# One core, 2,196 tasks in a written order: the order written anew, with 49 fewer tasks that only keep TensorE running

## The chip, the cores and the metric

The kernel runs on one core of a Trainium2 chip. A core has TensorE (PE in the profile: matmuls; PEld: the loading of its stationary operand), VectorE (DVE), ScalarE (ACT), GpSimd (POOL) and SyncE (SP, which here only issues DMAs). The engines run each its own queue in order and wait for one another by semaphores. The metric is the device time of one execution in microseconds; three runs of the kernel before took 638.27, 638.80 and 639.24 us, median 638.8 us.

## What is computed

A delta rule over 768 steps in each of 32 heads (4 batches of 8 heads, head size 48), and its output, seen as 3,072 tokens of 384 features, goes through a feed-forward block whose gate is h cos h:

```python
k_n = k / (np.linalg.norm(k, axis=-1, keepdims=True) + 1e-06)
for t in range(S):
    y[:, :, t] = np.einsum('bhd,bhde->bhe', q[:, :, t], state)
    v_old = np.einsum('bhde,bhd->bhe', state, kt)
    state = state + bt[:, :, :, None] * np.einsum('bhd,bhe->bhde', kt, vt - v_old)
...
h = x @ w_in          # x: 3072 x 384, w_in: 384 x 2048
g = h * np.cos(h)
return g @ w_out      # w_out: 2048 x 384
```

The weights arrive as 64-bit floats and are narrowed on the chip.

## The kernel before

**Delta rule.** The 768 steps are cut into 24 units n of 32 steps. For a unit, `turn` transposes keys and queries on TensorE (units 0 to 7; later units are loaded in blocks and turned on VectorE), `turn_out` evicts them, `gram` multiplies keys with keys and queries (line 673), `gram_keys` and `gram_queries` scale and mask the products on VectorE. Each unit then needs the inverse of a triangular 32 x 32 matrix per head:
- units 0 and 1 by `double`: six levels of small matmuls (L757), in two halves (`par`) each, and between the levels `double_copy` on ScalarE and `double_turn` and `double_add` on VectorE (L765 to L777);
- units 2 and 3 by a half-size substitution, with `solve_half`, `between` and `solve`;
- units from 4 on in pairs m = n // 2 by substitution on GpSimd: `gram_put` writes the matrices to DRAM, `gram_get` reads both units' back in another layout (L852), `inv` m, 0 to 6 does 31 columns of two instructions (L877, L884), `put` writes the result (L889) and `get` reads it per unit (L908).

Then come `state` (product with the running state, L928), `right` (VectorE), `solve` (L994, L1000), `solve_out`, `update` (L1025) and `update_out` (the new state), `within` and `within_out` (the unit's outputs) and `features` and `features_out` (transposed, as input of the feed-forward block). `update_out` n must precede `state` n + 1: this is the only chain through all units.

**Feed-forward block.** Two units make one tile p of 256 tokens, 12 tiles in all. Tiles 0 and 1 go through plain matmuls (`hidden`, L1097); the others through 20 shared products (`layer`, L1271). `turns`, `rest`, `cos` and `gate` (ScalarE and VectorE in turn) make h cos h; `out` (L1353; L1295 for tile 0) is the second matmul, from tile 1 on in seven products of two parts. `x_sum`, `left`, `right`, `in_sums` are sums of operands on VectorE or GpSimd.

**Weights.** 28 pieces: `weights` t loads, `split` t (ScalarE, two instructions), `shift` t (VectorE), `add` t (GpSimd) narrow it. `hidden` 0, f needs `add` up to 3 (f // 2 % 4) + 2, and `out` 0, 0, k needs `add` 12 to 15 + 4k.

**Order.** All this is a list of tasks. Each has a key such as `("gram", 5)`. `Order.LINE` lists the numbers of all tasks; `run` emits them in this order, and since each engine's queue is in order, the list fixes what stands behind what on every engine. It also fixes which buffer a task gets. `Order.OTHER` holds the keys of tasks that go to a second engine instead of their first: DMAs to ScalarE's queue instead of SyncE's, `inv`, `left`, `right`, `in_sums` and `x_sum` to the other of VectorE and GpSimd.

**Unread products.** `keep_warm` (lines 491 to 493) multiplies two tiles of ones into `p_out`, which nobody reads. `WARM_FIRST` = 5 of them are emitted ahead of the list, and `WARMS` tasks `("warm", i)` stand in the list. Each `warm` task that comes after the first `out` task emits nothing (`out_begun` is then not empty). Before, 31 of the 56 stand ahead of the first `out`.

Of the kernel before, what the change touches and what calls it, by code (L numbers as in the profile page):

```python
# [59 lines left out]
class Order:  # L60

    OTHER = {
        ('gram_put', 2), ('q', 3), ('gram_get', 1), ('inv', 1, 0), ('put', 1), ('gram_put',
        4), ('gram_put', 5), ('v', 7), ('v', 8), ('v', 9), ('blocks', 11, 1), ('gram_put',
        11), ('put', 5), ('v', 13), ('put', 6), ('gram_put', 15), ('gram_get', 7), ('get',
        15), ('v', 16), ('blocks', 16, 0), ('blocks', 16, 1), ('gram_put', 16), ('blocks',
        18, 1), ('k', 19), ('blocks', 19, 0), ('gram_get', 9), ('get', 19), ('gram_put',
        20), ('v', 21), ('gram_put', 21), ('put', 10), ('gram_put', 22), ('v', 23),
        ('gram_put', 23), ('gram_get', 11), ('right', 4, 4), ('left', 1, 1, 0), ('left', 1,
        3, 0), ('left', 1, 3, 1), ('store', 1, 0), ('x_sum', 2, 'd'), ('x_sum', 2, 'n'),  # L70
        ('x_sum', 2, 'm'), ('x_sum', 2, 'e'), ('x_sum', 2, 'k'), ('x_sum', 2, 'g'),
        ('x_sum', 2, 'i'), ('x_sum', 2, 'l'), ('x_sum', 2, 'f'), ('x_sum', 2, 'b0'),
        ('left', 2, 4, 1), ('left', 2, 3, 1), ('x_sum', 3, 'd'), ('x_sum', 3, 'n'),
        ('x_sum', 3, 'm'), ('x_sum', 3, 'e'), ('x_sum', 3, 'k'), ('x_sum', 3, 'g'),
        ('x_sum', 3, 'i'), ('x_sum', 3, 'l'), ('x_sum', 3, 'h'), ('x_sum', 3, 'b0'),
        ('left', 3, 4, 1), ('left', 3, 3, 1), ('x_sum', 4, 'd'), ('x_sum', 4, 'm'),
        ('x_sum', 4, 'g'), ('x_sum', 4, 'i'), ('left', 4, 3, 0), ('left', 4, 3, 1),
        ('store', 4, 0), ('x_sum', 5, 'd'), ('x_sum', 5, 'e'), ('x_sum', 5, 'l'), ('x_sum',
        5, 'h'), ('x_sum', 5, 'b0'), ('left', 5, 2, 0), ('left', 5, 4, 1), ('left', 5, 3,
        0), ('left', 5, 3, 1), ('store', 5, 0), ('x_sum', 6, 'd'), ('x_sum', 6, 'g'),  # L80
        ('x_sum', 6, 'l'), ('x_sum', 6, 'f'), ('x_sum', 6, 'b0'), ('left', 6, 1, 0),
        ('left', 6, 4, 0), ('store', 6, 1), ('x_sum', 7, 'd'), ('x_sum', 7, 'm'), ('x_sum',
        7, 'g'), ('x_sum', 7, 'i'), ('x_sum', 7, 'f'), ('x_sum', 7, 'h'), ('x_sum', 7,
        'b0'), ('left', 7, 4, 0), ('left', 7, 4, 1), ('left', 7, 3, 1), ('x_sum', 8, 'd'),
        ('x_sum', 8, 'm'), ('x_sum', 8, 'e'), ('x_sum', 8, 'k'), ('x_sum', 8, 'g'),
        ('x_sum', 8, 'l'), ('left', 8, 3, 0), ('store', 8, 0), ('store', 8, 1), ('x_sum', 9,
        'd'), ('x_sum', 9, 'm'), ('x_sum', 9, 'e'), ('x_sum', 9, 'k'), ('x_sum', 9, 'i'),
        ('x_sum', 9, 'l'), ('x_sum', 9, 'b0'), ('left', 9, 1, 0), ('left', 9, 2, 0),
        ('left', 9, 1, 1), ('left', 9, 3, 0), ('store', 9, 0), ('x_sum', 10, 'k'), ('x_sum',
        10, 'i'), ('x_sum', 10, 'l'), ('x_sum', 10, 'h'), ('x_sum', 10, 'b0'), ('left', 10,  # L90
        1, 0), ('left', 10, 1, 1), ('left', 10, 4, 1), ('left', 10, 3, 0), ('left', 10, 3,
        1), ('store', 10, 0), ('x_sum', 11, 'd'), ('x_sum', 11, 'e'), ('x_sum', 11, 'k'),
        ('x_sum', 11, 'g'), ('x_sum', 11, 'f'), ('left', 11, 1, 0), ('left', 11, 2, 0),
        ('left', 11, 1, 1), ('left', 11, 3, 0), ('left', 11, 3, 1), ('store', 11, 1),
        ('store_right', 11), ('weights', 5), ('weights', 7), ('weights', 15), ('weights',
        16), ('weights', 18), ('weights', 20), ('weights', 22), ('weights', 23), ('weights',
        25), ('weights', 27)
    }

    WARM_FIRST, WARMS = 5, 56  # L100
    LINE = """
# [1845 lines left out]
```

## Time and profile before

| | us |
|---|---|
| median of three runs | 638.8 |
| span of the profiled execution, first to last instruction | 636.6 |
| TensorE busy, and of it the unread products (72 rows: 36 products of two rows) | 619.2, 23.1 |
| TensorE's weight loading busy | 576.2 |
| VectorE, GpSimd, ScalarE busy | 495.1, 435.8, 297.7 |

A row of the trace is one instruction: line of the kernel, engine, operation, the tiles it writes and reads, start and duration. An fp32 matmul of this kernel is two rows. "Idle before" is the time for which the engine had nothing to run ahead of a group, with what ended it.

### The profile page before, as it was taken

Reading aid. Unit: us, or ns where it says so; the run is one execution under the profiler, and the core shown is the slowest. Engines: PE = TensorE matmul, PEld = TensorE weight load, DVE = VectorE, ACT = ScalarE, POOL = GpSimd, SP = SyncE. Lnnn points to the kernel's source line nnn. Section 1 sums busy time; section 2 is a strip of 40 time slices with the busy share of each in tenths; the row PEclk is TensorE's granted clock in tenths of the full one; section 3 lists DMA queues with packets and bytes.
Section 4 is the critical chain, followed back from the end, with each engine's and each line's share of the span. In section 5 each row is a group of like instructions: output and inputs, shape, how many; then the busy total and the mean of one; then the engine's idle time right before and its main releaser. Section 6 shows DMA issues by size and latency. Waiting matters only on the chain.

```text
span 636.6 us, 24189 instructions
## 1 busy us (share of the span) xinstructions
PE 619.2 (97%) x10176; PEld 576.2 (90%) x10176; DVE 495.1 (78%) x1030; ACT 297.7 (47%) x528; POOL 435.8 (68%) x780
## 2 busy tenths in 40 slices
PE   5999989999999999999999999999999999999997
PEld 4877877987899999999999999999999999999997
DVE  5776656779998999887898888888888776566682
ACT  3457556562423444643642644733643553545440
POOL 5247788678788788887789888886884883112241
PEclk8899999999999999999999999999999999999999
DMA  8978656563651555435435344333304102000001
GB/s 173 221 171 213 121 155 146 93 118 60 116 68 22 94 90 99 60 67 104 61 70 98 56 73 90 58 57 67 74 3 81 44 1 43 19 2 26 1 25 26
DMA packets 209381, 50.37 MB, mean 79 GB/s; under 512 B 200920, under 2 KB 204280, under 8 KB 209272
## 3 DMA queue, kind: packets, MB, share of 16 engines
q1 hardware_dynamic: 161896, 35.03, 29.3%
q10 hardware_dynamic: 47072, 13.25, 10.0%
q8 instruction: 80, 1.31, 0.9%
q0 software_dynamic: 304, 0.54, 0.4%
q14 instruction: 29, 0.24, 0.1%
HBM read 38.55 MB, written 10.22 MB: 77 GB/s over the span
## 4 chain that ended last, share of the span: by engine, by line
PE 90%; DVE 3%; DMA 3%; ACT 1%; issue 1%; POOL 0%; SPq 0%; ACTq 0%; DVEq 0%
PE p_out L1353 29%; PE p_h L1271 27%; PE p_h L1097 6%; PE p_kq L928 4%; PE p_out L1295 3%; PE p_s L1025 3%; PE p_g L673 3%; PE p_h L757 3%; PE p_kq L1055 3%; PE p_u L1000 3%; PE p_out L493 2%; PE p_h L1353 2%; PE p_z L1076 1%; DMA kp<-in_k_dram 1%; PE p_t L640 1%
## 5 line engine op out<-in xcount | busy, mean ns | idle before, releaser
L877 POOL TENSOR_TENSOR part<-z,gb 128x126 f32<-128x126 f32 (+23 forms) x321 | 144.6, 451 | 46.7 <-DMA gb<-g_dr 21.2
L884 POOL TENSOR_TENSOR z<-z,part 128x126 f32<-128x126 f32 (+23 forms) x321 | 145.5, 453 | 25.1
L1353 PE MATMUL p_out<-w_out,g_ffn 128*128 128x192 f32 x672 | 121.9, 328 | 0.3 <-DVE o L1405 0.2
L1353 PEld LDWEIGHTS p_out<-w_out,g_ffn 128*128 128x128 f32 x672 | 107.7, 190 | 1.7 <-DVE o L1405 0.7
L1150 ACT ACTIVATE turns<-turns,halfpi 128x512 f32<-128x512 f32 x96 | 68.0, 719 | 55.7 <-DVE turns L1141 42.6
L1353 PE MATMUL p_out<-w_sum,g_ffn 128*128 128x192 f32 x496 | 89.7, 329 | 0.2 <-DVE o L1405 0.2
L1271 PE MATMUL p_h<-x_sum,w_in 128*128 128x128 f32 x640 | 84.0, 277 | 0.0
L1134 ACT ACTIVATE turns<-g_ffn,quarter_turn 128x512 int32<-128x512 f32 x70 | 49.8, 719 | 66.4 <-DVE g_ffn L1288 31.3
L1353 PEld LDWEIGHTS p_out<-w_sum,g_ffn 128*128 128x128 f32 x496 | 79.6, 190 | 1.2 <-issue 0.4
L1271 PEld LDWEIGHTS p_h<-x_sum,w_in 128*128 128x128 f32 x640 | 78.8, 192 | 1.1
L1288 DVE TENSOR_TENSOR g_ffn<-g_ffn,p_h 128x512 f32<-128x512 f32 x80 | 54.3, 681 | 17.3 <-PE p_h L1271 16.4
L1141 DVE SCALAR_TENSOR_TENSOR turns<-g_ffn,turns 128x512 f32<-128x512 f32 x70 | 55.3, 796 | 13.1 <-ACT turns L1134 13.0
L1068 ACT COPY y<-p_kq 32x384 f32<-32x384 f32 x96 | 45.2, 470 | 30.4 <-PE p_kq L1055 22.5
L1153 DVE TENSOR_TENSOR g_ffn<-turns,g_ffn 128x512 f32<-128x512 f32 x70 | 51.5, 745 | 3.8 <-ACT turns L1150 3.7
L1271 PE MATMUL p_h<-x_sum,in_sum 128*128 128x128 f32 x400 | 52.9, 277 | 0.0
L572 POOL TENSOR_TENSOR knrm<-ksum,halves 128x16 f32<-128x16 f32 (+1 forms) x14 | 36.4, 2602 | 23.9 <-DMA qp<-in_q_dram 12.6
L1271 PEld LDWEIGHTS p_h<-x_sum,in_sum 128*128 128x128 f32 x400 | 49.7, 192 | 0.8
L1405 DVE SCALAR_TENSOR_TENSOR o<-p_out,o 128x192 f32<-128x192 f32 x74 | 25.1, 351 | 28.4 <-PE p_out L1353 28.0
L1097 PE MATMUL p_h<-x_ffn,w_in 128*128 128x128 f32 x384 | 45.8, 277 | 0.0
L1097 PEld LDWEIGHTS p_h<-x_ffn,w_in 128*128 128x128 f32 x384 | 44.1, 192 | 1.2
L1271 PE MATMUL p_h<-x_ffn,w_in 128*128 128x128 f32 x320 | 42.4, 277 | 0.0
L1369 POOL TENSOR_TENSOR g_ffn<-g_ffn,g_ffn 128x512 f32<-128x512 f32 x18 | 25.8, 1442 | 22.5 <-PE p_out L1353 18.7
(168 smaller groups left out, 1071.3 us busy)
## 6 DMA issues: line engine op xcount, KB each, us to landing
g_ffn<-in_moe_w_in_dram SPq DMA_DIRECT2D x10, 512.0 KB
gb<-g_dr SPq DMA_DIRECT2D x14, 256.0 KB
vp<-in_v_dram SPq DMA_DIRECT2D x68, 48.0 KB
g_ffn<-in_moe_w_out_dram SPq DMA_DIRECT2D x8, 384.0 KB
g_ffn<-in_moe_w_out_dram ACTq DMA_DIRECT2D x8, 384.0 KB
kp<-in_k_dram SPq DMA_DIRECT2D x120, 24.0 KB
out_dram<-o SPq DMA_DIRECT2D x14, 192.0 KB
zt<-z_dr SPq DMA_DIRECT2D x72, 32.0 KB
```

Source lines behind the costliest of these rows:

```text
L572: nc.gpsimd.tensor_tensor(out=scales[m][2][:, part], in0=sums[m, part.start][:, 0:n], in1=halves[:, 0:n], op=ALU.pow,)
L877: eng.tensor_tensor(out=part, in0=z[:, 0:rows, j, None].to_broadcast(shape), in1=a[:, j, None, j + 1 :].to_broadcast(shape), op=ALU.mult,)
L884: eng.tensor_tensor(out=behind, in0=behind, in1=part, op=ALU.subtract)
L1068: nc.scalar.copy(by_parity(y[quarter(b)]), p_kq[quarter(b ^ 1), :, b % 2])
L1097: nc.tensor.matmul(p_h[:, i], w_in[:, t, (4 * k + i) * 128 : (4 * k + i + 1) * 128], xts[p][:, t, unit * 128 : (unit + 1) * 128], start=(i ...
L1134: nc.scalar.activation(turns[p, f], hidden_of(p, f), AF.Identity, bias=quarter_turn, scale=TURN)
L1141: nc.vector.scalar_tensor_tensor(out=r, in0=hidden_of(p, f), scalar=TURN, in1=t, op0=ALU.mult, op1=ALU.subtract,)
L1150: nc.scalar.activation(r, r, AF.Sin, bias=halfpi, scale=2.0 * math.pi)
L1153: nc.vector.tensor_tensor(out=place(p, f), in0=step_of(rests.pop((p, f)), f), in1=step_of(hidden_of(p, f), f), op=ALU.mult,)
L1271: nc.tensor.matmul(p_h[:, e], in_block(*w)[:, e], x_of(p, b), start=new and e == 0, stop=True, skip_group_check=True,)
L1288: nc.vector.tensor_tensor(out=part_of(p, to), in0=part_of(p, one), in1=part_of(p, two), op=op)
L1353: nc.tensor.matmul(p_o, left(p, part, a)[:, e % 4], right(e, b), start=(e == 0), stop=(e == FT // 2 - 1), skip_group_check=True,)
```

## The change

The tasks, their instructions and their data stay as they are, but for the unread products. `OTHER` loses 38 keys and gains 35, all of them of DMAs: each of these moves from one queue to another (SyncE's or ScalarE's). The choice between VectorE and GpSimd is the same for every task. `WARMS` falls from 56 to 7, so the tasks after these are numbered 49 lower, and all 2,147 places of `LINE` are written anew. All seven `warm` tasks stand ahead of the first `out`.

```diff
     OTHER = {
-        ('gram_put', 2), ('q', 3), ('gram_get', 1), ('inv', 1, 0), ('put', 1), ('gram_put',
-        4), ('gram_put', 5), ('v', 7), ('v', 8), ('v', 9), ('blocks', 11, 1), ('gram_put',
...
+        ('q', 2), ('inv', 1, 0), ('q', 5), ('gram_put', 5), ('v', 6), ('q', 7), ('gram_get', 3),
+        ('put', 3), ('gram_put', 8), ('blocks', 9, 0), ('blocks', 10, 1), ('gram_put', 10),
...
+        ('weights', 0), ('weights', 1), ('weights', 2), ('weights', 3), ('weights', 4),
+        ('weights', 9), ('weights', 10), ('weights', 11), ('weights', 14), ('weights', 16),
+        ('weights', 17), ('weights', 20), ('weights', 21), ('weights', 25)
     }
 
-    WARM_FIRST, WARMS = 5, 56
+    WARM_FIRST, WARMS = 5, 7
     LINE = """
-0 1 66 2 70 2084 3 71 4 8 9 72 122 67 68 5 2085 123 69 127 73 128 124 65 75 125 80 76 77 2088 178 78
...
+0 17 18 1 21 19 2 5 20 22 23 24 26 3 4 27 129 2035 73 130 78 2039 2036 158 74 2043 25 8 9 10 28 31
...
```

Put into names, TensorE's queue from its first product on is, before:

```
turn 0, warm 0-1, gram 0, turn 1, double 0,0,1 0,0,0, gram 1, warm 2, double 0,1,0 1,0,0, warm 3-4,
double 0,1,1 1,1,0, warm 5-7, double 0,2,0, warm 8-9, double 0,2,1 1,0,1, turn 2, warm 10-11,
double 1,1,1, turn 3, double 0,3,0 0,3,1, warm 12, gram 2, warm 13, double 1,2,0, warm 14-15,
double 0,4,1, warm 16-17, gram 3, double 0,4,0, warm 18-19, double 1,2,1 0,5,0 0,5,1, turn 4, warm 20,
solve 0, ...
```

and after:

```
turn 0, gram 0, turn 1, warm 0-2, double 0,0,0 0,0,1, turn 2, double 0,1,0, gram 1, double 0,2,0 0,1,1,
warm 3, double 1,0,1, gram 2, double 0,2,1 0,3,0 1,0,0 0,4,0, warm 4, double 0,3,1 1,1,1 1,1,0 0,4,1,
turn 3, double 0,5,0, gram 3, double 1,2,1 0,5,1, turn 4, double 1,2,0, solve 0, ...
```

(`double` n, level, half.)

More of the change, by code (lines that the diff above doesn't have):

```diff
@@ L62 @@
     OTHER = {
-        ('gram_put', 2), ('q', 3), ('gram_get', 1), ('inv', 1, 0), ('put', 1), ('gram_put',
-        4), ('gram_put', 5), ('v', 7), ('v', 8), ('v', 9), ('blocks', 11, 1), ('gram_put',
[L65 to L97, printed above, removed]
+        ('q', 2), ('inv', 1, 0), ('q', 5), ('gram_put', 5), ('v', 6), ('q', 7), ('gram_get', 3),
+        ('put', 3), ('gram_put', 8), ('blocks', 9, 0), ('blocks', 10, 1), ('gram_put', 10),
@@ new lines @@
+        ('get', 11), ('v', 12), ('gram_get', 6), ('put', 6), ('get', 13), ('v', 14),
+        ('blocks', 16, 1), ('v', 17), ('blocks', 18, 0), ('blocks', 18, 1), ('get', 18),
+        ('k', 19), ('blocks', 19, 1), ('gram_get', 9), ('v', 20), ('gram_put', 21),
+        ('gram_get', 11), ('right', 4, 4), ('left', 1, 1, 0), ('left', 1, 3, 0),
+        ('left', 1, 3, 1), ('x_sum', 2, 'd'), ('x_sum', 2, 'n'), ('x_sum', 2, 'm'),
+        ('x_sum', 2, 'e'), ('x_sum', 2, 'k'), ('x_sum', 2, 'g'), ('x_sum', 2, 'i'),
@@ new lines @@
+        ('x_sum', 2, 'l'), ('x_sum', 2, 'f'), ('x_sum', 2, 'b0'), ('left', 2, 4, 1),
+        ('left', 2, 3, 1), ('x_sum', 3, 'd'), ('x_sum', 3, 'n'), ('x_sum', 3, 'm'),
+        ('x_sum', 3, 'e'), ('x_sum', 3, 'k'), ('x_sum', 3, 'g'), ('x_sum', 3, 'i'),
+        ('x_sum', 3, 'l'), ('x_sum', 3, 'h'), ('x_sum', 3, 'b0'), ('left', 3, 4, 1),
+        ('left', 3, 3, 1), ('x_sum', 4, 'd'), ('x_sum', 4, 'm'), ('x_sum', 4, 'g'),
+        ('x_sum', 4, 'i'), ('left', 4, 3, 0), ('left', 4, 3, 1), ('x_sum', 5, 'd'),
@@ new lines @@
+        ('x_sum', 5, 'e'), ('x_sum', 5, 'l'), ('x_sum', 5, 'h'), ('x_sum', 5, 'b0'),
+        ('left', 5, 2, 0), ('left', 5, 4, 1), ('left', 5, 3, 0), ('left', 5, 3, 1),
+        ('store', 5, 0), ('x_sum', 6, 'd'), ('x_sum', 6, 'g'), ('x_sum', 6, 'l'),
+        ('x_sum', 6, 'f'), ('x_sum', 6, 'b0'), ('left', 6, 1, 0), ('left', 6, 4, 0),
+        ('store', 6, 0), ('x_sum', 7, 'd'), ('x_sum', 7, 'm'), ('x_sum', 7, 'g'),
+        ('x_sum', 7, 'i'), ('x_sum', 7, 'f'), ('x_sum', 7, 'h'), ('x_sum', 7, 'b0'),
@@ new lines @@
+        ('left', 7, 4, 0), ('left', 7, 4, 1), ('left', 7, 3, 1), ('store', 7, 0),
+        ('x_sum', 8, 'd'), ('x_sum', 8, 'm'), ('x_sum', 8, 'e'), ('x_sum', 8, 'k'),
+        ('x_sum', 8, 'g'), ('x_sum', 8, 'l'), ('left', 8, 3, 0), ('store', 8, 0),
+        ('store', 8, 1), ('x_sum', 9, 'd'), ('x_sum', 9, 'm'), ('x_sum', 9, 'e'),
+        ('x_sum', 9, 'k'), ('x_sum', 9, 'i'), ('x_sum', 9, 'l'), ('x_sum', 9, 'b0'),
+        ('left', 9, 1, 0), ('left', 9, 2, 0), ('left', 9, 1, 1), ('left', 9, 3, 0),
@@ new lines @@
+        ('store', 9, 1), ('x_sum', 10, 'k'), ('x_sum', 10, 'i'), ('x_sum', 10, 'l'),
+        ('x_sum', 10, 'h'), ('x_sum', 10, 'b0'), ('left', 10, 1, 0), ('left', 10, 1, 1),
+        ('left', 10, 4, 1), ('left', 10, 3, 0), ('left', 10, 3, 1), ('store', 10, 1),
+        ('x_sum', 11, 'd'), ('x_sum', 11, 'e'), ('x_sum', 11, 'k'), ('x_sum', 11, 'g'),
+        ('x_sum', 11, 'f'), ('left', 11, 1, 0), ('left', 11, 2, 0), ('left', 11, 1, 1),
+        ('left', 11, 3, 0), ('left', 11, 3, 1), ('store', 11, 1), ('store_right', 11),
```

195 rows, old and new, of the table LINE are left out of this document.

## The prediction

> **What bounds the kernel now.** First the page, to see whether one engine is the bound:
>
> ```profile
> span 636.6 us, 24189 instructions
> ...
> PE   5999989999999999999999999999999999999997
> ...
> PEclk8899999999999999999999999999999999999999
> ```
>
> TensorE runs at nine tenths or more nearly throughout, at the full clock but for the first two slices. So the time is what TensorE must do plus what it loses, and the question is where it loses. Busy time by stretch (first columns: length, then TensorE, its weight loading, VectorE, ScalarE, GpSimd):
>
> ```profile
> 14.80:59.00 44.20, 42.27 (x847) 34.16 (x847) 34.01 (x105) 23.16 (x48) 20.03 (x20) 0.93 0.84 198
> 59.00:112.00 53.00, 49.00 (x1209) 43.26 (x1198) 33.32 (x69) 32.54 (x64) 44.09 (x83) 1.00 0.63 146
> 112.00:600.00 488.00, 486.99 (x7826) 460.18 (x7826) 399.87 (x799) 227.25 (x394) 352.79 (x655) 1.00 0.35 62
> ```
>
> From 112 us to the end TensorE idles 1.0 us in 488: no order of VectorE and GpSimd can win anything there. Ahead of it TensorE looks full, but part of that is the unread product of line 493 (duration min/median/max in ns, first and last start):
>
> ```profile
> L493 PE MATMUL p_out<-o x72: 379/379/796, 1.3 to 88.1; 128*128 128x256 f32 x72
> ```
>
> They are busy for 23.05 us, all before 89 us. With 619.24 us of TensorE busy, the work that is read takes 619.24 - 23.05 = 596.2 us, and the span holds 636.6 - 596.2 = 40.4 us of loss: 6.1 before the first real product, 3.6 after the last, and some 30 between, nearly all before 112 us. Was anything ready when an unread product ran? The timelines of TensorE and, below it, VectorE (start, length):
>
> ```profile
> 24.55 1.56 PE L493 MATMUL p_out<-o 128*128 128x256 f32 x6
> 26.04 1.09 PE L757 MATMUL p_h<-in_sum 64*64 64x128 f32 x16
> ```
> ```profile
> 23.93 0.77 DVE L773 STREAM_TRANSPOSE in_sum<-p_h 128x256 f32<-128x256 f32 x2
> ...
> 29.27 0.45 DVE L773 STREAM_TRANSPOSE in_sum<-p_h 128x256 f32<-128x256 f32 x1 [1.35 <-PE p_h L757]
> ```
>
> Yes: level 2 of `double` (26.04) needed the first of the two transposes at 23.93, done by 24.4, and stood behind three unread products until 26.04. VectorE then sat idle for 1.35 us waiting for TensorE. So in the start-up the fill itself stretches the chain.
>
> **The change, part by part.** *Unread products.* 31 in the list become 7: 24 go. Those 31 took 23.05 - 3.84 (the first five) = 19.2 us, so 24/31 of it, 14.9 us, leaves TensorE. That is not yet a gain: where nothing was ready, the wait remains.
>
> *Order of the start-up.* Up to 14.88 nothing moves: `gram_keys` 0 waits for the norms in both (VectorE's `scale` 0 ends at 12.50), and level 0 starts at 14.88. From there VectorE sets the pace. From 14.83 to `double_add` 0,5,1 inclusive its tasks, at their durations before, sum to 23.6 us before (38.4 if it never waited; it ended at 45.45, so 7.0 us of waits: 0.92, 0.89, 1.35, 0.99, 0.68, 0.58 and smaller) and to 22.6 after. I walked the new queues by hand with the durations of before (VectorE add or turn 0.42, both halves of the eye subtraction 1.28, `scale` 1.09, `shift` 0.42; TensorE level 0.6 or 1.05, twice that at half clock until 21.3; `turn` 1.09, `gram` 0.86). Ends of level 1, 2, 3, 4 of half 0: 20.4, 22.5, 29.2, 30.8 against 21.0, 27.1, 34.2, 41.9 before; last add 41.1; `solve` 0 starts at 43.0 (47.09), as `turn` 1,1,0 and `double` 1,2,0 stand ahead of it; `update_out` 0 ends at 48.9 (51.5); `hidden` 0,0 starts at 54.8 (59.05), `solve` 1 at 57.7 (64.06), `gram` 5 at 65.1 (68.54), `state` 2 at 66.0 (73.57). `solve` 2 comes at 80 against 81.45, with 5.7 us more of products by their rows done ahead of it (`hidden` 0,6 and 0,8 come earlier), some 5.5 us net of the rows' overlap. So the start-up is worth 81.45 + 5.5 - 80 = **7.0 us**. Floor: the fill cost nothing (0). Ceiling: VectorE never waits, last add at 37.4 instead of 41.1, 10.7 us.
>
> *DMAs.* `weights` 0 to 4 and `q` 2 (four DMAs) move to ScalarE's queue, nine issues of some 0.45 us, between 9 and 21 us. Behind them stand `split` 0, `turn_out` 1 and the `double_copy`s; ScalarE sat idle for 0.76, 1.21, 2.61 and 1.98 us there, which covers the 4 us; without that cover each us would make level 1 late by as much, 4 us at most. `q` 5 and `weights` 9 stand ahead of `split` 8 and `within_out` 0; ScalarE's idle 2.92 us before `within_out` 0 covers their five issues (2.3 us); without it `features` 0 and `hidden` 0,0 would be late by these. SyncE loses these issues, and `k` 2 to `k` 4 come earlier by what `weights` 0 to 3 took. I price the queues at nothing.
>
> *VectorE and GpSimd apart.* `add` 5 took 1.87 us where its like take 1.29, beside `weigh` on VectorE. A collision spared is 0.6 us on GpSimd, hidden by TensorE's products after 112 us. Without that cover every such us would come out at the end. Priced at nothing.
>
> *Inverse of the first full pair.* This is what is late next. `solve` 4 needs `inv` 2, `put` 2 and `get` 4, which start from `gram` 5. Before, `solve` 4 came 64.3 us after `gram` 5; now only 54.8 us of products by their rows stand between, which overlap by some 4% (60.4 by rows were 58.2 net of 6.1 us fill and idle), so 52.8. The chain: `gram` 5 to `inv` 2,0 11.4, since GpSimd has its `add`s and `norms` to do until 76.5 (before 12.7; least of any pair 10.8); `inv` 2: 33.6 with four `add`s of 1.0 before, 29.5 bare, now with seven, 36.7; then `put`, `get`. Before:
>
> ```profile
> 121.58 0.39 SPq L831 DMA_DIRECT2D g_dr<-g  x1
> 122.07 0.53 SPq L889 DMA_DIRECT2D z_dr<-z  x1
> ...
> 125.58 2.92 SPq L908 DMA_DIRECT2D zt<-z_dr  x4
> ```
>
> The inverse ended at 114.9 but its `put` stood at 122.07 behind `gram_put` 7. Now `gram` 7 comes at 105, so `gram_put` 7 is gone in time: `put` to the first `get` 3.5 us as here, four issues 1.9, and 1.9 to land, as the 1.97 us of another small transfer on the chain of waits: 7.3. Sum 11.4 + 36.7 + 7.3 = 55.4 against 52.8: TensorE waits **2.6 us**. Ends: 0 and, with the 18.0 us that it took from `inv` 2,6 to `solve` 4 before, 13.3. Pair 3 has 54.0 x 0.96 = 51.8 and needs 12.5 + 31 + 7.3 = 50.8: no wait. From pair 4 on the distances are 56.8 to 65.6 by rows, against 59.7 to 65.9 before.
>
> *Tail.* The last products stand in the same order: 0.
>
> **Sum.** 636.6 - 7.0 + 2.6 = 632.2 us of span. The median run is 2.2 us over the profiled span, so **634.4 us**.
>
> **Rivals.**
> *A, no wait at `solve` 4 and a start-up nearer its ceiling.* For: TensorE idles nowhere after 112 us now. Against: pair 2 has 11 us less room. 638.8 - 7 = 631.8, at the ceiling 628.1.
>
> *B, the gain is swallowed.* If the walk is right but VectorE waits as long as before (7.0 us instead of 41.1 - 37.4 = 3.7 or less), 3 to 4 us go and the wait at `solve` 4 eats most of the rest: 637.5 to 640. For: every step above leans on durations of another order.
>
> *C, slower: the inverse of pair 2.* If `put` and `get` 4 take 13 to 18 us after `inv` 2,6, as for most pairs before (10.6 to 18.0), TensorE stands at `solve` 4 for 8.3 to 13.3 us: 640.1 to 645.1. It decides from 11.7 us on (52.8 + 7.0 - 11.4 - 36.7). For it: 36.7 us of GpSimd work that cannot be shortened. Against: TensorE never waited for these pairs, so the 10.6 to 18.0 hold slack.
>
> *D, slower: the clock.* The windows of the start (granted clock is the third column from the end):
>
> ```profile
> 7.64:11.05 3.41, 1.78 (x71) 1.29 (x71) 1.80 (x4) 2.50 (x6) 1.67 (x1) 1.00 1.03 240
> ...
> 14.47:17.88 3.41, 3.00 (x96) 2.72 (x96) 3.31 (x12) 0.98 (x3) 0.11 (x1) 0.50 0.74 170
> 17.88:21.29 3.41, 3.41 (x34) 2.74 (x30) 2.85 (x7) 1.43 (x4) 0.00 (x0) 0.50 1.05 239
> 21.29:24.70 3.41, 3.41 (x49) 2.79 (x46) 2.98 (x8) 2.08 (x5) 0.00 (x0) 1.00 0.96 216
> ```
>
> After a stretch with TensorE busy for 1.78 of 3.41 us the clock fell to half, and it came back only after a stretch busy throughout. With 24 products fewer, stretches of 70 to 75% occur again (I find 2.45 of 3.4 us at 24.7 to 28.1). Half clock doubles TensorE's share of the chain, 0.5 us lost per us; it turns the sign from 4.4 / 0.5 = 8.8 us of extra half clock on. 15 us would give 634.4 + 7.5 = 641.9. Against: at half clock TensorE is fuller, which brings the clock back.
> The Trainium skill (TensorE: Matmul & The Clock Gate, "HAM oscillation — how this bites in real kernels") has the clock fall only where TensorE is idle for more than about 3.4 us; by it there would be no loss, since no gap of the walk is over 2 us. This trace differs: its longest gap before the fall at 11.05 was 1.6 us.
>
> **How the numbers follow.** Forecast 634.4 with 0.53 (its own range 631 to 637.4), A 0.20, B 0.11, C 0.09, D 0.07. The range 627 to 642 takes in A whole and the near ends of C and D. About 0.2% (1.3 us) is what a measurement of this kernel can tell from no change: faster, under 637.5, holds the forecast, A and a little of B, 0.74; within, B, 0.10; slower, C and D, 0.16.
>
> **What would show it.** Line 493 with 24 rows and 12 products; `hidden` 0,0 (first L1097) at 54 to 56 us; half clock ended by 21 to 25 us; TensorE busy for some 12 to 15 us less in sum; an idle of TensorE of 0 to 5 us at `solve` 4 (L1000, near 118 us), released by a DMA; 112 to 600 us as full as before. It is wrong if `hidden` 0,0 is not earlier than 58 us, if idle after 112 us sums to over 6 us, or if half clock goes on past 30 us.

## The result, and the profile after

The changed kernel takes 642.62 us (median of 12 runs, 639.52 to 646.25); the kernel before, beside it, 639.41 us (12 runs, 638.07 to 642.79). The ratio is 1.0051 with a 95% interval of 1.0027 to 1.0074: **slower by 0.5%**, where 0.7% faster was forecast. The profiled execution took 644.53 us with a span of 642.7, so it lies 1.9 us above the median; its mean granted clock, 0.994, is the highest of the twelve, whose median is 0.984 (kernel before: 0.995).

The page after: span, TensorE and its clock in 40 slices of 16.1 us, and the shares of the chain that ended last.

```profile
span 642.7 us, 24095 instructions
...
PE   7778989989999999899999999999999999999997
...
PEclk9997999999999999999999999999999999999999
...
PE 66%; DMA 11%; POOL 9%; DVE 6%; SPq 3%; issue 2%; ACT 1%; ACTq 0%; POOLq 0%; DVEq 0%
```

Two things are new: the clock falls in the fourth slice (48 to 64 us) instead of the first two, and a fifth of the chain now runs over DMAs and GpSimd (before: DMA 3%, DVE 3%, PE 90%). The unread products did go, from 72 rows to 24:

```profile
L490 PE MATMUL p_out<-o x24: 379/570/796, 1.3 to 63.6; 128*128 128x256 f32 x24
```

(This kernel's text is three lines shorter ahead of the functions, so L490, L886, L905, L997 and L1094 here are L493, L889, L908, L1000 and L1097 of before.) Busy time by stretch, as before: length, then TensorE, its weight loading, VectorE, ScalarE, GpSimd, and the granted clock third from the end.

```profile
50.00:60.00 10.00, 8.46 (x179) 7.27 (x179) 5.11 (x22) 3.70 (x9) 5.74 (x13) 0.66 0.69 183
...
112.00:160.00 48.00, 44.27 (x889) 37.30 (x889) 35.81 (x71) 21.35 (x38) 40.47 (x85) 1.00 0.56 96
160.00:320.00 160.00, 156.78 (x2687) 146.53 (x2664) 139.60 (x292) 68.36 (x120) 125.51 (x240) 1.00 0.47 79
...
480.00:600.00 120.00, 118.53 (x1521) 115.28 (x1521) 84.52 (x155) 55.28 (x95) 49.19 (x88) 1.00 0.15 30
```

Behind 112 us TensorE idles 3.73 + 3.22 + 1.47 = 8.4 us, where it idled 1.0 us before. What it waited for there, the longest line (us in sum, times, longest):

```profile
PE p_u L997 <- DMA zt<-z_dr: 7.0, 6, 2.1
```

L997 is `solve`, and `zt` is the inverse as `get` reads it. It waited at `solve` 4 (130.0 us, 2.94 us), `solve` 10 (259.1 us, 2.59 us) and `solve` 22 (534.7 us, 1.47 us): pairs 2, 5 and 11. In the start-up the first place that goes otherwise than walked is this one (TensorE's timeline: start, length, in brackets the idle time before it and what ended it):

```profile
47.81 1.45 PE L754 MATMUL p_h<-w_sum 64*64 64x64 f32 x32
51.54 1.22 PE L490 MATMUL p_out<-o 128*128 128x256 f32 x2 [2.27 <-DVE bz L593]
52.55 0.85 PE L1073 MATMUL p_z<-consts,y 128*128 128x128 f32 x3
...
59.34 2.94 PE L1094 MATMUL p_h<-x_ffn,w_in 128*128 128x128 f32 x24
```

An unread product, `warm` 5, itself waits for 2.27 us: it writes `p_out`, and `scale` 2,0 uses a part of `p_out` as scratch (`spare_out`). `features` 0 (52.55) stands behind it, the granted clock is at half from 51.1 to 57.9 us, and `hidden` 0,0 begins at 59.34 us.

**Where the time went.** Count the needed products that TensorE has done at an instant, each at its kind's median start-to-start time before, and subtract that from the instant; the difference between two kernels is how far one is ahead. In profiled executions, one of each kernel, against the kernel before (plus: ahead, us; a single entry is good to about 1 us):

| kernel | at 60 us | 112 | 160 | 262 | 540 | 630 |
|---|---|---|---|---|---|---|
| changed | +0.8 | +3.7 | -0.8 | -4.3 | -5.9 | -6.0 |
| new start, old rest (e4) | +2.8 | +4.2 | +1.4 | +1.2 | +1.1 | +1.1 |
| old start, new rest (e5) | -0.2 | +0.1 | -8.0 | -7.9 | -11.2 | -11.4 |
| changed, puts first (g1) | -0.3 | +2.4 | -0.1 | -1.8 | -1.9 | -1.9 |
| changed, more fill (g3) | +5.3 | +7.5 | +2.0 | -2.2 | -3.3 | -3.3 |
| new start, old rest, mended, filled (e12, second time) | +5.2 | +9.0 | +4.3 | +4.3 | +4.2 | +4.4 |

The start-up did win 3.7 us in this execution (in e4 and g1, which begin with the same start, 4.2 and 2.4). Then 9.7 us go: 7.4 of them are the idle time above (8.4 less the 1.0 of before), and the other 2.3 us are spread over the rows and were not traced further.

### The profile page after: what moved, and what is told of

It reads as the page before. It is cut to its first block, busy times and chain, and to the rows that moved or that the text cites. A ratio compares the mean times of both kernels' runs of the same rounds, so it can differ in the third digit from the quotient of the medians.

```text
span 642.7 us, 24095 instructions
## 1 busy us (share of the span) xinstructions
PE 612.5 (95%) x10128; PEld 571.6 (89%) x10128; DVE 496.0 (77%) x1030; ACT 296.3 (46%) x528; POOL 426.7 (66%) x780
## 3 DMA queue, kind: packets, MB, share of 16 engines
q10 hardware_dynamic: 40220, 15.02, 10.5%
## 4 chain that ended last, share of the span: by engine, by line
PE 66%; DMA 11%; POOL 9%; DVE 6%; SPq 3%; issue 2%; ACT 1%; ACTq 0%; POOLq 0%; DVEq 0%
PE p_h L1268 23%; PE p_out L1350 23%; DMA z_dr<-z 4%; POOL z L881 4%; PE p_h L1094 4%; POOL part L874 3%; DMA kp<-in_k_dram 3%; PE p_kq L925 2%; PE p_s L1022 2%; PE p_u L997 2%; PE p_kq L1052 2%; PE p_g L670 2%; PE p_h L1350 2%; PE p_out L1292 1%; DMA zt<-z_dr 1%
## 5 line engine op out<-in xcount | busy, mean ns | idle before, releaser
L874 POOL TENSOR_TENSOR part<-z,gb 128x126 f32<-128x126 f32 (+23 forms) x321 | 140.5, 438 | 46.8 <-DMA gb<-g_dr 17.7
L881 POOL TENSOR_TENSOR z<-z,part 128x126 f32<-128x126 f32 (+23 forms) x321 | 142.3, 443 | 25.2
L1350 PE MATMUL p_out<-w_out,g_ffn 128*128 128x192 f32 x672 | 120.6, 328 | 0.1
L1150 DVE TENSOR_TENSOR g_ffn<-turns,g_ffn 128x512 f32<-128x512 f32 x70 | 55.5, 800 | 16.0 <-ACT turns L1147 15.9
L1138 DVE SCALAR_TENSOR_TENSOR turns<-g_ffn,turns 128x512 f32<-128x512 f32 x70 | 52.4, 758 | 9.6 <-ACT turns L1131 9.6
L1094 PE MATMUL p_h<-x_ffn,w_in 128*128 128x128 f32 x384 | 46.6, 278 | 0.1
L569 POOL TENSOR_TENSOR knrm<-ksum,halves 128x16 f32<-128x16 f32 (+1 forms) x14 | 36.4, 2598 | 13.4 <-DVE ksum L557 13.3
L1094 PEld LDWEIGHTS p_h<-x_ffn,w_in 128*128 128x128 f32 x384 | 44.0, 192 | 1.3 <-issue 0.2
L1366 POOL TENSOR_TENSOR g_ffn<-g_ffn 128x512 f32<-128x512 f32 x15 | 20.0, 1334 | 35.4 <-DVE g_ffn L1150 30.1
```

The source lines that it names most:

```text
L569: nc.gpsimd.tensor_tensor(out=scales[m][2][:, part], in0=sums[m, part.start][:, 0:n], in1=halves[:, 0:n], op=ALU.pow,)
L874: eng.tensor_tensor(out=part, in0=z[:, 0:rows, j, None].to_broadcast(shape), in1=a[:, j, None, j + 1 :].to_broadcast(shape), op=ALU.mult,)
L881: eng.tensor_tensor(out=behind, in0=behind, in1=part, op=ALU.subtract)
L1094: nc.tensor.matmul(p_h[:, i], w_in[:, t, (4 * k + i) * 128 : (4 * k + i + 1) * 128], xts[p][:, t, unit * 128 : (unit + 1) * 128], start=(i ...
L1138: nc.vector.scalar_tensor_tensor(out=r, in0=hidden_of(p, f), scalar=TURN, in1=t, op0=ALU.mult, op1=ALU.subtract,)
L1150: nc.vector.tensor_tensor(out=place(p, f), in0=step_of(rests.pop((p, f)), f), in1=step_of(hidden_of(p, f), f), op=ALU.mult,)
```

## The experiments

Each kernel ran beside the kernel before on the same chip. `LINE` is a list of numbers, so the edits are shown in the names of the tasks. A ratio is to the kernel before that ran beside it, with its 95% interval; the changed kernel's own is 1.0051 [1.0027, 1.0074]. The experiments used five chips, on which the kernel before took 638.8 to 640.4 us in the median, so between kernels of different experiments the ratios say more than the difference in us.

### Is it the missing fill? (e1)

The order before, with 7 of its 31 unread tasks:

```diff
 turn 0, warm 0-1, gram 0, ..., warm 5-6,
-double 0,2,0, warm 7-9, double 0,2,1 1,0,1, turn 2, warm 10-11, ...
+double 0,2,0, double 0,2,1 1,0,1, turn 2, ...
```

> The order before, with only its first seven tasks of unread products left (24 emitted products fewer) and nothing else changed. Theory (the inverse's chain): the products dropped all lie ahead of 60 us, where PE waits mostly for data, so at most the 0.2 to 1 us that a dropped product itself held up a needed one comes back: 637.5 to 640 us, waits of PE after 112 us about 1 us as before. The clock rival (fewer unread products lower the clock, and that is what made the changed kernel slower): a second stretch at half clock appears between 25 and 60 us, hidden 0,0 comes 2 us or more later than 59 us, 641.5 us or more. Third: the unread products stood in the way of needed ones, 636.5 us or less.

639.41 us, ratio 0.9984 [0.9969, 0.9998]. A second stretch at half clock did appear (40 to 52 us, granted clock 0.50 to 0.67), as the clock rival had it, and yet the kernel is no slower: its three runs with a mean granted clock of 0.984 to 0.986, as low as the changed kernel's, took 639.45 to 639.75 us. By 49 us the profiled run was as far as the kernel before (0.3 us ahead). So less fill alone costs nothing, and it wins about 1 us at most, not 7: that gain needs the new order of the start.

### The unread product that waits (e2)

```diff
 double 1,4,1, double 1,4,0, scale 2,0,
-warm 5,
 features 0
```

> The changed kernel without the one task of two unread products at 51.5 us, which waited 2.27 us for a scratch write of VectorE; all else in its order. Theory: features 0 begins at about 50.2 us instead of 52.6, the clock does not fall at 51 us, hidden 0,0 begins at 54.5 to 57 us instead of 59.3, and PE leads the kernel before by 3 to 5 us at 60 us instead of 0.8; but the solves of pairs 2, 5 and 11 still wait, for up to as much more as PE comes earlier, so the end gains only 0 to 3 us: 639.5 to 642.6 us, waits for the inverse 7 to 11 us in sum. Rival (the unread product kept the clock up and its wait is hidden behind others): the clock still falls near 51 us, hidden 0,0 at 59 us or later, 642.6 us or more.

642.61 us, ratio 1.0052 [1.0034, 1.0071]: nothing gained. `features` 0 began at 50.02 us as expected and `hidden` 0,0 at 57.30, but 1.55 us of idle time remained ahead of `features` 0 (it waits for ScalarE's `within_out` 0), and the clock fell all the same (0.50 from 52 to 56 us). The expectation that the clock would hold was wrong; that the end would gain 0 to 3 us was right at its low edge, with 5.9 us of waits for the inverse left (expected: 7 to 11).

### Move the waiting solves (e3, e7)

```diff
-out 0,0,2, solve 4, hidden 1,8, update 4, within 4, out 0,0,3, features 4
+out 0,0,2, hidden 1,8, solve 4, out 0,0,3, update 4, within 4, features 4
...
-out 2,5,0, solve 10, layer 4,18, out 2,5,1, update 10
+out 2,5,0, layer 4,18, out 2,5,1, solve 10, layer 4,15, out 2,6,0, update 10
...
-out 8,4,1, solve 22, out 8,5,0, layer 10,18
+out 8,4,1, out 8,5,0, layer 10,18, solve 22
```

> The changed kernel with solve 4, solve 10 and solve 22 each moved behind one to three products of work that waits for nothing (solve 4 behind hidden 1,8; solve 10 behind out 2,5,1; solve 22 behind layer 10,18; what hangs on them follows, and the fetch of get 5 that needs its buffer), all else in its order. Theory: the three waits for the fetched inverse (2.9, 2.6 and 1.5 us) shrink to under 2.5 us in sum, and 4 to 7 us come back: 635.5 to 638.5 us. Rival one (the later order is worse as a whole, the waits only show where the time surfaces): the stall moves to the next task of the chain, waits of PE after 112 us stay at 7 us or more, 641.5 to 643 us. Rival two (the clock): no wait remains but the time stays, 641 us or more.

> The changed kernel with both edits: without the two unread products at 51.5 us and with solves 4, 10 and 22 moved later. Theory: PE comes 2 to 4 us earlier to solve 4, so part of the wait there returns (its inverse does not come earlier by as much); solves 10 and 22 wait under 1 us each: 633 to 638 us, at or below the lower of the two edits alone. Rival (one cause behind both, so the two edits do not add): the same time as the better of the two alone, with a wait for the inverse of pair 2 that is longer by what the start gained.

647.14 us (ratio 1.0106 [1.0084, 1.0127]) and, without `warm` 5, 644.65 us (1.0072 [1.0055, 1.0088]): the first is slower than the changed kernel, the second no faster, and the theory as it stood fell. TensorE's waits after 112 us in the first of them:

```profile
PE p_out L1350 <- DVE o L1402: 2.8, 2, 2.3
PE p_z L1073 <- DVE st L1030: 2.3, 1, 2.3
PE p_h L1094 <- ACT x_ffn L1081: 1.7, 1, 1.7
```

No wait for the inverse is left in this list, but 6.8 us of others are: at `hidden` 1,8 (129.6 us), `features` 4 (140.4 us) and `out` 2,6,0 (263.5 us). The products that I pulled ahead of a solve were the cover of the next links, `update` to `features` and `out`; moved ahead, they cover nothing there. A late input is not mended by moving the task that waits; the input has to come earlier.

### Which half loses? (e4, e5, e6)

```diff
+ LINE, OTHER of the changed kernel up to ("within", 3)   # about 113 us
+ then all other tasks in the relative order of the kernel before, with its OTHER
```

(e5: the other way round; e6: e4 without `warm` 5.)

> The changed kernel's order and queues up to within 3 (about 113 us), and from there the relative order and queues of the kernel before; seven tasks of unread products as in the changed kernel. Theory (the start's lead is real and the later order gives it back): PE reaches within 3 about 3.7 us ahead of the kernel before and keeps 2 to 4 us of it, waits of PE after 113 us under 3 us in sum: 636 to 638 us. Rival one (the lead is lost at pairs 2 and 3 whatever the later order is, because their inverses were begun in the start and come no earlier): solve 4 or 6 waits 2 to 4 us, 639 to 641 us. Rival two (the clock): granted clock near 0.984 in the median and 641 us or more.

> The other half: the order and queues of the kernel before up to within 3, with its unread products, and from there the changed kernel's relative order and queues. Theory (the later order is what loses): solve 4 waits less than 1.5 us since PE comes 3.7 us later, solves 10 and 22 wait 2 to 4 us in sum, and some 2 us go between 112 and 160 us: 642 to 645 us with a granted clock of about 0.994. Rival one (the later order is no worse, its waits only hand back a lead that the chain cannot hold): 638.5 to 640.5 us. Rival two (the clock makes the difference between the two kernels): 638.5 to 640.5 us too, told from rival one by the kernel with the new start and the old rest, which then is slower than the kernel before.

> The kernel with the new start and the old rest, without the two unread products at 51.5 us as well. Theory: another 2 us of lead at 60 us, of which the wait for the inverse of pair 2 takes 1 to 2 back: 634.5 to 637 us, not slower than the same kernel with those products. Rival (no clock without them): half clock after 49 us, the same time as with them or more.

e4: 637.65 us, ratio 0.9977 [0.9963, 0.9990], faster than the kernel before. e5: 648.49 us, 1.0148 [1.0129, 1.0168], slower than the 642 to 645 us expected. e6: 638.72 us, 0.9996 [0.9973, 1.0019], no gain over e4, against the expectation. So the new start wins and **the new rest loses**: 0.74% with the new start ahead of it (1.0051 against 0.9977). In e5 it seems to lose twice that, but there most goes at the seam (8 of 11 us between 112 and 160 us in the table): the inverse of pair 2 took 46.0 us on GpSimd from `inv` 2,0 to `inv` 2,6, against 33.6 before, among the `add`s of another order.

### Queues and order belong together (e8)

```diff
 LINE of the changed kernel
-OTHER of the changed kernel
+OTHER of the kernel before
```

> The changed kernel's order with each transfer on the queue that the kernel before issued it from (46 transfers go back from one queue to the other). If the new queues are what makes the put and get of an inverse late (3.2 to 7.3 us from put to first get, 3.1 to 5.4 before), the waits for the inverses of pairs 2, 5 and 11 fall from 7.0 to under 3 us and the time to 637 to 640 us. If the order itself asks too early, the waits stay at 5 us or more in sum: 641.5 to 644 us.

(38 keys go back one way and 35 the other, not the 46 that the expectation names.) 668.22 us, ratio 1.0454 [1.0422, 1.0485]. Neither expectation held: the very same tasks in the same order are 26 us slower with the other kernel's choice of queue. The prediction had priced the queues at nothing. In this kernel the waits for the inverse are those of pairs 2, 3 and 10 (1.43, 1.03 and 2.52 us); where the rest of the 26 us goes was not traced. At pair 5, whose `put` is back on ScalarE's queue, 3.9 us pass from `put` to the first `get` and the solve waits 0.12 us. So order and queues cannot be priced apart; that the new queues as a whole cost the changed kernel anything is not shown.

### A shorter inverse (f1, and f2 as control)

Six of the 31 columns of the inverse are left out, so these kernels do not compute the inverse; they only measure its length.

```diff
         for j in columns:
+            if m > HALVED and j in (9, 10, 11, 13, 14, 15):
+                continue
             rows, last = (j + 1, HC) if m == HALVED else (j // SPLIT + 1, C)
```

> The changed kernel with part of the inverse left out: 6 of the 31 columns of the elimination of pairs 2 to 11 (columns 9, 10, 11, 13, 14 and 15, two instructions each, 120 instructions of some 0.45 us on GpSimd or VectorE), so that each inverse is some 5 us shorter; order and queues unchanged. Theory (the later order asks for the inverse too early, and only that): the waits for the inverse, 7.0 us in sum, fall under 0.5 us, and nothing else takes their place: 634 to 637 us. Rival (whatever follows the solve is the next to be late, as when the three solves alone were moved; or the later order loses elsewhere): the time falls by less than 3 us, 640 us or more.

> Control: the kernel before with the same 120 instructions of the inverse left out. Theory: there every solve is reached 6.2 to 8.8 us after the last fetch is issued and none waits, so a shorter inverse is worth nothing: 637.5 to 640 us. If it gains 2 us or more, a lighter GpSimd or VectorE is worth time by itself, and that has to be taken off what the changed kernel gains by the same cut.

f1: 640.15 us, 1.0006 [0.9986, 1.0025]; f2: 639.23 us, 0.9993 [0.9978, 1.0008]. The control is as expected: before, a shorter inverse is worth nothing. In the changed kernel it brings 2.5 us (642.62 - 640.15; 2.9 us by the ratios), not the 6 to 8 forecast. The waits say why:

```profile
PE p_u L999 <- DMA zt<-z_dr: 5.1, 4, 2.8
```

The wait at `solve` 22 is gone, but `solve` 4 still waits 3.71 us. In f1 the inverse of pair 2 ended 4.8 us before its `put` was issued (3.5 us in the changed kernel), that of pair 3 9.8, of pair 4 9.8 and of pair 5 7.0. SyncE's queue in f1, one row for issues in a row (start, time for issuing):

```profile
113.27 0.39 SPq L828 DMA_DIRECT2D g_dr<-g  x1
113.71 2.88 SPq L393 DMA_DIRECT2D vp<-in_v_dram  x4
116.63 3.13 SPq L412 DMA_DIRECT2D qp<-in_q_dram  x4
119.86 0.43 SPq L888 DMA_DIRECT2D z_dr<-z  x1
```

and in the changed kernel itself:

```profile
115.79 3.12 SPq L393 DMA_DIRECT2D vp<-in_v_dram  x4
118.95 2.98 SPq L412 DMA_DIRECT2D qp<-in_q_dram  x4
122.03 0.68 SPq L886 DMA_DIRECT2D z_dr<-z  x1
127.06 1.79 SPq L905 DMA_DIRECT2D zt<-z_dr  x4
```

Between the transfer that begins the next pair (`g_dr`) and the `put` of this one (`z_dr`) stand eight issues, `v` 5 and `blocks` 8,1, which take 6 us of SyncE, back to back. The inverse was done at 118.6 us; its `put` goes out at 122.0. Then it needs 5.0 us until the first `get` (3.5 before), with the 192 KB of `blocks` 8,1 issued just ahead of it.

### The puts ahead of bulk loads (g1, g2)

```diff
-gram_put 7, v 5, blocks 8,1, put 2, get 4, k 11
+gram_put 7, v 5, put 2, get 4, blocks 8,1, k 11
...
-gram_put 13, blocks 15,0, put 5, get 10, k 16
+gram_put 13, put 5, get 10, blocks 15,0, k 16
```

(SyncE's queue. g2 has this and the shorter inverse.)

> The changed kernel with two transfers issued later on SP's queue: blocks 8,1 (which is issued for 3.0 us right ahead of the put of pair 2's inverse) behind get 4, and blocks 15,0 (3.4 us right ahead of the put of pair 5's) behind get 10; all else in its order. Theory (put and get come late because they stand behind bulk transfers, in the queue and in the transfer itself): the put of pair 2 is issued 2 to 3 us earlier, the 6.3 us from put to first get of pair 5 shrink to about 3.5 us, the waits at solves 4 and 10 fall from 5.5 to under 2 us in sum, and 2 to 4 us come back: 638.5 to 641 us. Rival (the next link of the chain is late as well, as when the solves were moved): less than 1.5 us comes back, 641.5 us or more.

> Both: those two transfers behind the gets, and the 120 instructions of the inverse's columns 9, 10, 11, 13, 14 and 15 left out as before. Theory (the waits for the inverse are what the later order loses): with inverse and queue both out of the way the waits at solves 4, 10 and 22 are under 1 us in sum, and the time is 635 to 638 us, below the short inverse alone by 2 us or more. Rival: the time stays at 639.5 us or more, that is, the later order and the clock lose the rest without any wait for the inverse.

g1: **639.01 us**, 0.9996 [0.9973, 1.0019]; g2: **636.08 us**, 0.9952 [0.9927, 0.9977]. Two transfers moved on one queue bring 3.6 us (3.5 by the ratios), about as much as leaving out 6 of the inverse's 31 columns (2.5 and 2.9 us; the intervals overlap). In g1 the `put` of pair 2 stands right behind `v` 5 and goes out as the inverse ends, and 3.7 us later comes the `get`:

```profile
117.13 2.48 SPq L393 DMA_DIRECT2D vp<-in_v_dram  x4
120.33 0.39 SPq L886 DMA_DIRECT2D z_dr<-z  x1
124.02 2.20 SPq L905 DMA_DIRECT2D zt<-z_dr  x4
126.27 2.04 SPq L412 DMA_DIRECT2D qp<-in_q_dram  x4
```

Pair 5 goes from 6.3 us between `put` and `get` to 4.8 (expected 3.5). In the changed kernel its rows are

```profile
250.46 0.38 SPq L886 DMA_DIRECT2D z_dr<-z  x1
256.78 1.79 SPq L905 DMA_DIRECT2D zt<-z_dr  x4
```

and in the kernel before, where this `put` went out on ScalarE's queue (ACTq),

```profile
249.78 0.40 ACTq L889 DMA_DIRECT2D z_dr<-z  x1
252.86 1.80 SPq L908 DMA_DIRECT2D zt<-z_dr  x4
```

There 3.1 us lay between the two. The waits in g1, TensorE's longest two after 112 us:

```profile
PE p_z L1073 <- ACT y L1065: 1.5, 1, 1.5
PE p_u L997 <- DMA zt<-z_dr: 1.2, 2, 0.7
```

1.2 us where there were 7.0; in g2 no wait for the inverse of 0.2 us or more is left, and g2 is 6.5 us below the changed kernel (6.3 by the ratios), close to the 7.0 us of waits. This is the cause, shown from both sides: take the waits away, at the inverse or at the queue, and what the later order lost comes back, while the kernel before gains nothing from a shorter inverse (f2).

### Is it the clock? (g3)

```diff
-double 1,4,0, scale 2,0, warm 5, features 0
+double 1,4,0, warm, warm, scale 2,0, features 0
...
+warm, warm,
 gram 4
...
+warm,
 between 2
+warm, warm,
 solve 2
```

> The changed kernel with unread products put back where PE idles in the start: two tasks after double 1,4,0 instead of the one that waited at 51.5 us, two ahead of gram 4, one ahead of between 2, two ahead of solve 2 (12 more products, 2 of them in place of the 2 that waited). If the half clock that follows those idle stretches (51 to 58 us, in other runs 80 to 86 us) is what costs the changed kernel: median granted clock 0.990 or more instead of 0.984, and 1.5 to 4 us less, 638.5 to 641 us. If the clock is no more than a sign of PE's idle time: the clock rises, the time stays within 1 us, 641.6 us or more, and the waits at the solves grow by what the start gains.

641.88 us, 1.0048 [1.0027, 1.0068]. The median granted clock rose from 0.984 to 0.991 (before: 0.995), and the start is 7.5 us ahead at 112 us instead of 3.7, yet the time is the same. g1, on the same chip and with the same median clock of 0.991, took 639.01 us: at this clock the two transfers are worth 2.9 us. The changed kernel's profiled execution says so too: with half clock for 6.8 us in the start, against 10.2 us in the kernel before, its span is still 6.1 us longer (642.7 against 636.6). TensorE's waits after 112 us, the longest line:

```profile
PE p_u L998 <- DMA zt<-z_dr: 7.1, 6, 2.5
```

It arrives earlier and waits as long, and what the start gained is lost between 112 and 262 us. As long as the solves wait, a better start and a better clock bring nothing to the median. Where they hardly wait the clock does count: the six runs of g1 with a granted clock of 0.994 or 0.995 took 636.0 to 638.9 us, the five with 0.986 to 0.988 took 639.2 to 641.4, the one with 0.981 took 644.4.

Part of a low clock is itself an effect of the waits: in g3 the granted clock is 0.60 from 128 to 132 us and 0.51 from 257.5 to 261 us, just behind the waits at `solve` 4 and `solve` 10, and in e2 0.51 from 129 to 132.4 us. How much of the changed kernel's 3.2 us goes by way of the clock is open.

### A faster kernel (e10, e11, e12)

e4 idles 2.51 us at 113 us, ahead of `features` 3, where the order before has `out` 0,0,1 as cover, which the new start has done already:

```diff
-within 3, features 3, state 4, gram 7, hidden 1,2
+within 3, hidden 1,2, features 3, state 4, gram 7
```

e11 adds the two tasks after `double` 1,4,0 of g3 in place of `warm` 5, e12 also the other five of g3.

> The kernel with the new start and the old rest (faster than the kernel before by 0.2%), with hidden 1,2 moved ahead of features 3. There PE waited 2.5 us at 113 us for ScalarE's copy of the last output rows (p_z from y), since out 0,0,1, which covers that place in the kernel before, is done in the start. Theory: 1.5 to 2.5 us of that come back: 634.5 to 636.5 us. Rival (the stall goes on to state 4 or solve 4): 637 us or more, with the wait at that task.

> The mended kernel (new start, old rest, hidden 1,2 ahead of features 3) with the unread products of 51.5 us moved ahead of the scratch write that they waited for, two tasks instead of one (two more products), so that they fill PE's 1.6 us wait ahead of features 0 and wait for nothing themselves. If that idle time is what makes the granted clock fall at 51 us: no half clock between 50 and 60 us, hidden 0,0 by 57.5 us, 1 to 2.5 us faster than the same kernel without this edit, 633 to 635 us. If the clock falls for another reason, or PE has slack behind it: half clock at 51 us again or the same time within 1 us.

> The same unread products in the kernel with the new start, the old rest and the mended seam (where no solve waits for its inverse). If the clock costs time there: no half clock between 25 and 110 us, clock 0.993 or more in the median, 634 to 636 us, 1 us or more below the mended kernel without them (636.8 us). If not: within 0.8 us of it.

> The fastest kernel so far (new start, old rest, hidden 1,2 ahead of features 3, six more tasks of unread products) once more, beside the kernel before: ratio 0.991 to 0.997, 634.5 to 637 us. A ratio above 0.998 would say that the gain of 0.6% was chance.

e10: 636.84 us, 0.9945 [0.9921, 0.9968]; e11: 636.65 us, 0.9955 [0.9938, 0.9972]; e12: 635.96 us, 0.9939 [0.9915, 0.9963], and again 633.88 us, 0.9916 [0.9896, 0.9936]. All beat both kernels; e12 by 0.6 to 0.8% of the kernel before. The products added in e11 brought nothing that can be told (expected: 1 to 2.5 us). Those of e12 brought 0.9 us over e10 the first time and, by the ratios, 1.9 us the second (expected: 1 us or more); the intervals overlap with that of e10. In e11 TensorE's timeline at the place of the wait is now

```profile
47.64 1.13 PE L491 MATMUL p_out<-o 128*128 128x256 f32 x4
48.74 0.55 PE L1074 MATMUL p_z<-consts,y 128*128 128x128 f32 x3
...
54.64 2.94 PE L1095 MATMUL p_h<-x_ffn,w_in 128*128 128x128 f32 x24
```

and the windows show the clock held at 51 us, and lost from 81.3 us on, where TensorE waits 0.65, 0.73 and 1.61 us around `solve` 2:

```profile
50.00:60.00 10.00, 8.03 (x194) 7.04 (x189) 5.87 (x21) 5.19 (x10) 5.51 (x16) 1.00 0.85 213
...
80.00:90.00 10.00, 8.38 (x185) 7.76 (x186) 5.75 (x13) 2.50 (x5) 8.28 (x24) 0.66 0.72 175
```

### Both mends in the changed kernel (g4)

g1 and g3 together.

> The changed kernel with both: blocks 8,1 and blocks 15,0 issued behind the gets, and the unread products put back where PE idles in the start. Alone the first brought 3.6 us and the second nothing, although its start was 4 us ahead at 112 us. Theory (the start's lead was swallowed by the waits at the solves): with the waits mostly gone the lead is kept in part, 636 to 638.2 us, at least 1 us below the two transfers alone (639.0 us), and the waits for the inverse stay under 4 us in sum. Rival (the lead cannot be kept in this order, since its solves come 52 to 55 us of PE work after their products): 638.5 us or more, with 4 us or more of waits for the inverse.

638.52 us, 1.0008 [0.9984, 1.0032], from 632.9 to 644.1 us. Inconclusive: the profiled execution, the fastest at 632.90 us, has no wait for the inverse and ends 5.5 us ahead of the kernel before (spans of 631.1 and 636.6 us); the median gains nothing that can be told over g1. So this order can keep the lead, but does so in few executions. What differs between them stays open, since only one of them was profiled.

## Why the prediction was wrong

**The start-up** was walked rightly up to 49 us: `solve` 0 at 43.46 us (walked: 43.0; so in brackets from here on), and behind that in e11, where the wait that it had missed is gone and the clock holds: `hidden` 0,0 at 54.64 (54.8), `solve` 1 at 57.51 (57.7), `solve` 2 at 80.01 (80). The walk left out that unread products and `scale` 2 share `p_out`, and the second stretch at half clock (51.1 to 57.9 us): without the shared wait alone, in e2, `hidden` 0,0 still begins at 57.30. By 112 us 3.3 of the 7.0 us are missing; how they divide between the two was not measured. e2 shows that the wait cost the end of the changed kernel nothing, since the later waits took whatever came.

**The wait at `solve` 4** came out at 2.94 us (2.6), but its terms did not. The chain from `gram` 5 took 60.4 us, not 55.4: 13.8 to the inverse (11.4), 35.2 for it (36.7), 3.5 held in SyncE's queue (0, "`gram_put` 7 is gone in time"), 5.0 from `put` to `get` and 2.9 to the solve (7.3 in all). TensorE's own work up to that solve took 57.5 us, not 52.8. Two terms, each wrong by about 5 us, cancel: that the wait came out right is luck.

**The step that failed**, and with it the sign, is "From pair 4 on the distances are 56.8 to 65.6 by rows, against 59.7 to 65.9 before", which put the waits there at 0, together with "I price the queues at nothing". I held the distances against those of before and took the chain as unchanged. (Pair 3, with "no wait", was right.) The chain is longer (us, from the rows of the two profiled executions):

| | pair 5 before | changed | pair 11 before | changed |
|---|---|---|---|---|
| `gram` to the start of the inverse | 12.4 | 14.6 | 10.8 | 14.4 |
| the inverse | 34.2 | 33.8 | 34.3 | 36.5 |
| its end to the first `get` | 3.1 | 6.3 | 3.7 | 4.6 |
| first `get` to `solve` | 7.5 | 2.3 | 8.8 | 2.3 |
| `gram` to `solve` | 57.2 | 57.0 | 57.6 | 57.8 |
| of it, TensorE waits | 0 | 2.59 | 0 | 1.47 |

Up to the first `get` the chain grew by 4.9 us at pair 5 and by 6.8 at pair 11, while TensorE's work for that time grew shorter by only 2.8 and 1.3 us. In the kernel before the first `get` of every pair from 2 on was issued 6.2 to 8.8 us ahead of its solve, so there was room there that the changed kernel no longer has.

The 3.2 us that pair 5 lost between `put` and `get` belong to the queues: `put` 5 had moved from ScalarE's queue to SyncE's, behind `blocks` 15,0; with it back on the other queue (e8) 3.9 us pass to the `get`, with `blocks` 15,0 behind it (g1) 4.8, in the changed kernel 6.3. The transfers that I followed were those of the start; the eight issues ahead of `put` 2 I did not see, and they and `blocks` 15,0 are worth 3.6 us (g1).

**The sum.** The profiled span grew by 6.1 us where it was to shrink by 4.4. Of these 10.5 us, 3.3 are missing in the start-up, 4.1 are the waits at pairs 5 and 11, 0.3 the wait at pair 2, 0.4 other idle time, and some 2.3 us were not traced.

**Rival C** had the right kind of mechanism, an inverse that comes too late because of `put` and `get`, but put all of it on pair 2 (8.3 to 13.3 us, measured 2.94); that its times, 640.1 to 645.1 us, hold the measured one is luck. **Rival B** named the swallowed gain, by waits of VectorE and the one at `solve` 4; in g3 it is the waits at three solves that swallow it. **Rival D** (the clock) is refuted as what makes the kernel slower by itself: in e1 the clock fell without costing time, in g3 it rose without gaining any. A share of the loss by way of the clock stays open. **The tail** moved nothing, as said. TensorE's busy time fell by 6.8 us rather than 12 to 15: the unread rows fell by 13.5 us (23.1 to 9.5), nearly as forecast, but the needed rows were busy for some 5 us more than before, which was not traced. Of the signs of error that the text named, `hidden` 0,0 later than 58 us (59.34) and more than 6 us of idle time after 112 us (8.4) came true; half clock past 30 us came too, though as a second stretch.

The Trainium skill (DMA: Bandwidth & Descriptors, "Queues, rings and completion order") says that on each of the engines that carry a transfer the descriptors of a queue are consumed in the order of its ring. The runs agree: with `blocks` 15,0 taken from ahead of `put` 5 the time from `put` to `get` went from 6.3 to 4.8 us, and with `blocks` 8,1 taken from ahead of `put` 2 from 5.0 to 3.7. They do not tell the order within the queue from transfers that merely run at the same time.

## What to carry to other kernels

When an order is written anew, list for every long side chain the work that the bound engine has between its start and its consumer, and hold it against the whole chain, with its places in the DMA queues, not against the order before: here the chains of two pairs grew by 5 to 7 us, and the waits that followed cost more than a start-up 4 us shorter had won. A wait for a late input is mended at the input (here by issuing two bulk loads behind a `get` instead of ahead of its `put`), not by moving the waiting task, whose cover is needed next. And an order can be cut: the halves of two orders, spliced and run, show which half wins.

## What was not expected of the hardware

The granted clock falls after short idle times of TensorE. In the changed kernel the longest gap ahead of the fall at 51.1 us was 2.27 us, and the fall came before that gap had ended; in e2 the longest was 1.55 us, in e11 the gaps ahead of the fall at 81.3 us were 0.65, 0.73 and 1.61 us. The Trainium skill (TensorE: Matmul & The Clock Gate, "HAM oscillation — how this bites in real kernels") gives idle gaps over about 3.4 us as what does it; these traces differ. Filling one gap mends one fall only: e4, with the same start and no fill there, has falls at 50.1 and 84.3 us, e11 only the one at 81.3.

Which queue each transfer is issued from was worth 26 us here (e8), more than any order of the tasks that was tried.
